# Where the most used form of a run-time switch lies: another order for eight bodies of code

## The chip, the cores and the metric

One core of one Trainium2 chip runs the whole program. TensorE (PE) multiplies matrices; each multiplication stands in the trace as a load of weights (PEld) and a MATMUL. VectorE (DVE), ScalarE (ACT) and GpSimd (POOL) do the elementwise work; SyncE (SP) and POOL start most of the DMA transfers. Each engine has an instruction stream of its own, which is itself fetched from memory by DMA. The metric is the device time of one execution in microseconds (us), lower is better.

## What is computed

Two blocks in a row: an attention in which each position sees the first `n_global` keys and the last `n_local` ones, then a mixture of eight experts in which every token goes to one expert.

```
scores = scale * q @ k.T + bias            # 4 batches, 8 heads, 768 positions, 64 wide
scores = where(is_global | is_local, scores, -1e9)
x = softmax(scores) @ v                    # as 3072 tokens of 512
expert_idx = argmax(x @ w_gate)            # one of 8 experts for each token
for e in range(8):
    xe = x[expert_idx == e]
    out[expert_idx == e] = gate * (relu(xe @ w1[e]) @ w2[e])   # 512 -> 1024 -> 512
```

How many tokens an expert gets is known only at run time, some 384 of the 3072 each.

## The kernel before

The program is straight code with a hand-written order on every engine. The attention and the routing fill the first 170 us or so; rows of tokens are scattered into a buffer in DRAM, sorted by expert. From there on the eight experts follow one another, and this is the part that the change touches.

An expert's tokens are taken in three portions. Experts 0 and 1 have a first tile of 128 rows done early. Each expert then has a main part of 256 rows, which is always computed (`up_a`, `up_b`, `down_a`, `down_b`, in a Strassen-like scheme that needs sums of weights, `c1` and `c2`, made by DVE). What is left over, between 0 and 224 rows in steps of 32, is the *units*: a piece of 128 rows, one of 64 and one of 32, each present or not. So there are eight forms, numbered k = 0 to 7 by the three bits (4: the piece of 128; 2: that of 64; 1: that of 32). k = 5 is the form of 160 rows, k = 4 that of 128, k = 3 that of 96, k = 1 that of 32.

The form is chosen at run time. `table` (the line is quoted below) writes `k ^ ORDER` for every expert; `load_forms` brings the eight numbers into registers of PE and ACT, the only two engines whose code differs by form. `by_form` opens `tc.Switch`: in PE's stream and in ACT's stream there are eight bodies one behind the other, at equal distances, and the body that lies at place p holds the code of form `p ^ ORDER`. A branch at the end of the common code (line 1316 in the profile, the *dispatch*) jumps to the body, and a branch at the body's end (line 1316 too, the *exit*) jumps to the code behind, which is common to all forms again. Between the two branches PE issues the units' matmuls (lines 1107, 791, 801, 1118, 1132), with the main part's `down_a` (line 1025) mixed in; ACT issues the relus and copies that go with them.

```
nc.vector.tensor_scalar(self.form[:], k_i[:], ORDER, None, ALU.bitwise_xor)
```

```
for k in tc.Switch({eng: self.forms[e] for eng in self.ENGINES}, FORMS, hint=f"units{e}"):
    self.units(e, k ^ ORDER, between)
```

`hint(e)` gives PE alone a prefetch hint for the dispatch of expert e. Each body begins with a hint for its own exit, on both engines (line 1148).

Behind the exit of expert e, these follow, and the steps of the prediction name them by line:

- PE: `x_in(e + 1)` (line 943, eight transposes), `down_b(e)` (line 1034), then the next expert's `up_a` and `up_b` (line 963). The first `up_b` adds into the same PSUM bank that `up_a(0)` filled, and waits until DVE's first `up_add` (line 994) has read that bank.
- ACT: `gated` (line 1045, two multiplications of one half of the result by the gate), then the next expert's `up_copy` (line 990).
- DVE: `down_sums` (line 1041), the copies of the next expert's tokens (945), `x_combine` (953 to 956), one `y_out` (1055) that needs `gated`, `c1[3]` (923), three more `y_out` (1055, 1052, 1055), behind expert 1 also the eleven small instructions of `judge` (1268 to 1281), and then the next expert's `up_add` (994).
- POOL: the scatters of finished rows (725) and the gathers of the next ones (717); SP: the next but one expert's weights, 4 MB, into the buffers that expert e has just given up.

Of the kernel before, what the change touches and what calls it, by code (L numbers as in the profile page):

```python
# [23 lines left out]
def kernel(  # L24
# [636 lines left out]
    NS = 2  # L661
    SP1 = 32
    FORMS = 8
    ORDER = 6

    HF = NFC // 2
    HD = NDC // 2
# [3 lines left out]
    class Experts:  # L671
# [177 lines left out]
        def table(self):  # L849
# [29 lines left out]
            nc.vector.tensor_copy(out=k_i[:], in_=k[:])  # L879
            nc.vector.tensor_scalar(self.form[:], k_i[:], ORDER, None, ALU.bitwise_xor)  # L880
            bits_i = T([P, 3, E], I32, name="bits_i")
# [265 lines left out]
        def by_form(self, e, between):  # L1147
            for k in tc.Switch({eng: self.forms[e] for eng in self.ENGINES}, FORMS, hint=f"units{e}"):
                self.units(e, k ^ ORDER, between)
            if e + 1 < E:  # L1150
# [170 lines left out]
```

## Time and profile before

| | us |
|---|---|
| median of 4 runs | 521.41 |
| lowest and highest of them | 520.22 and 523.12 |
| the profiled execution, whole | 522.21 |
| its span in the trace | 520.4 |
| PE busy in the span | 502.0 |
| DVE busy | 327.8 |
| POOL busy | 189.9 |
| ACT busy | 147.4 |

The span is counted from the first to the last recorded instruction, so it is a little shorter than the execution's own time; 1.8 us lie around it. The granted TensorE clock was 0.995 over the span. In the trace the experts can be told by the shapes of the units' matmuls: expert 0 has the form of 96 rows, experts 1 and 7 that of 32, experts 2 and 4 that of 128, and experts 3, 5 and 6 that of 160.

In the timeline a line gives the start, the time from the first instruction's start to the last one's end, the engine, the line of the kernel, the operation with its tiles, a count, and in brackets how long the engine had been idle before and what the profile names as having ended that.

### The profile page before, as it was taken

Reading aid. Unit: us, or ns where it says so; the run is one execution under the profiler, and the core shown is the slowest. Engines: PE = TensorE matmul, PEld = TensorE weight load, DVE = VectorE, ACT = ScalarE, POOL = GpSimd, SP = SyncE. Lnnn points to the kernel's source line nnn. Section 1 sums busy time; section 2 is a strip of 40 time slices with the busy share of each in tenths; the row PEclk is TensorE's granted clock in tenths of the full one; section 3 lists DMA queues with packets and bytes.
Section 4 is the critical chain, followed back from the end, with each engine's and each line's share of the span. In section 5 each row is a group of like instructions: output and inputs, shape, how many; then the busy total and the mean of one; then the engine's idle time right before and its main releaser. Section 6 shows DMA issues by size and latency. Waiting matters only on the chain.

```text
span 520.4 us, 12430 instructions
## 1 busy us (share of the span) xinstructions
PE 502.0 (96%) x5035; PEld 423.7 (81%) x5035; DVE 327.8 (63%) x688; ACT 147.4 (28%) x298; POOL 189.9 (36%) x285
## 2 busy tenths in 40 slices
PE   7999999999996999999999999999999999999994
PEld 4888888888885778679899788969969868996983
DVE  5898998997994647727788168227617705822741
ACT  3554555555542101212212112102202211211120
POOL 5441161161163465315374055024316304502503
PEclk9999999999998999999999999999999999999999
DMA  9977699798941322046093452028164107400101
GB/s 184 210 156 164 163 213 238 162 264 198 360 176 43 122 69 67 9 173 246 21 325 113 162 216 66 2 108 321 40 232 181 26 1 278 160 2 24 42 5 50
DMA packets 96333, 72.77 MB, mean 140 GB/s; under 512 B 79324, under 2 KB 79326, under 8 KB 96228
## 3 DMA queue, kind: packets, MB, share of 16 engines
q1 hardware_dynamic: 87808, 52.44, 36.1%
q0 software_dynamic: 7872, 19.01, 10.7%
q8 instruction: 55, 0.90, 0.8%
q14 instruction: 50, 0.41, 0.3%
q10 hardware_dynamic: 548, 0.02, 0.1%
HBM read 61.46 MB, written 14.73 MB: 146 GB/s over the span
## 4 chain that ended last, share of the span: by engine, by line
PE 78%; DVE 8%; issue 6%; DMA 5%; POOL 1%; POOLq 0%; SPq 0%; ACT 0%; DVEq 0%; ACTq 0%
PE u L963 18%; PE u L791 10%; PE d L1025 9%; PE d L1034 7%; PE u L801 7%; PE po L402 5%; PE sp L360 5%; DMA w<-in_moe_w_dram 3%; DVE p L374 3%; PE d L801 3%; PE u L1132 3%; PE u L1107 2%; PE pt L239 2%; PE pr L412 2%; PE t L943 2%
## 5 line engine op out<-in xcount | busy, mean ns | idle before, releaser
L1041 DVE TENSOR_TENSOR UV<-UV,d 128x512 f32<-128x512 f32 x8 | 5.5, 687 | 110.9 <-ACT yu L1135 81.3
L725 POOL DMA_INDIRECT out_dram<-ys,to_u x8 | 8.3, 1039 | 142.6 <-ACT yu L1135 87.6
L374 DVE TENSOR_TENSOR p<-sp,other 128x1024 f32<-128x1024 f32 x40 | 47.0, 1217 | 12.3 <-PE sp L360 10.8
L791 PEld LDWEIGHTS u<-xsT,w 128*128 128x128 f32 x448 | 50.9, 192 | 1.8 <-DVE c L933 1.2
L791 PE MATMUL u<-xsT,w 128*128 128x128 f32 x448 | 51.7, 276 | 0.0
L402 PE MATMUL po<-p,vt 128*64 128x128 f32 x704 | 47.6, 283 | 2.3 <-DVE kt L244 2.2
L963 PE MATMUL u<-cx,c 128*128 128x128 f32 x384 | 48.1, 275 | 0.0
L402 PEld LDWEIGHTS po<-p,vt 128*64 128x64 f32 x704 | 39.0, 140 | 9.0 <-DVE kt L244 5.0
L381 ACT ACTIVATE p<-p 128x1024 f32<-128x1024 f32 (+1 forms) x48 | 45.0, 978 | 3.9 <-DVE p L374 2.8
L963 PEld LDWEIGHTS u<-cx,c 128*128 128x128 f32 x384 | 45.5, 192 | 0.0
L360 PE MATMUL sp<-qt,kt 64*128 64x128 f32 x448 | 38.1, 276 | 2.3 <-DVE kt L244 1.7
L963 PE MATMUL u<-xT,w 128*128 128x128 f32 x256 | 39.4, 277 | 0.0
L801 PE MATMUL u<-w,huT 128*128 128x512 f32 x80 | 35.1, 592 | 0.0
L963 PEld LDWEIGHTS u<-xT,w 128*128 128x128 f32 x256 | 34.2, 192 | 0.9 <-DVE cx L956 0.2
L360 PEld LDWEIGHTS sp<-qt,kt 64*128 64x128 f32 x448 | 31.1, 188 | 4.1 <-issue 2.3
L296 POOL COPY ka<-kt 128x384 f32<-128x384 f32 x16 | 8.1, 504 | 69.3 <-DVE den_all L436 66.9
L1025 PE MATMUL d<-c,ch 128*128 128x256 f32 x128 | 32.9, 379 | 0.0
L217 POOL DMA_INDIRECT xs_dram<-xr,slot_i x24 | 25.2, 1051 | 16.9 <-DVE cnt L853 11.0
L801 PEld LDWEIGHTS u<-w,huT 128*128 128x128 f32 x80 | 15.2, 190 | 17.0 <-issue 16.7
L242 ACT ACTIVATE qt<-pt 128x512 f32<-128x512 f32 x24 | 14.4, 598 | 51.8 <-PE pt L239 51.8
L390 DVE TENSOR_TENSOR pb<-p 128x512 f32<-128x512 f32 x40 | 28.9, 764 | 0.0
L1025 PEld LDWEIGHTS d<-c,ch 128*128 128x128 f32 x128 | 24.4, 190 | 3.3
(255 smaller groups left out, 1031.2 us busy)
## 6 DMA issues: line engine op xcount, KB each, us to landing
w<-in_moe_w_dram SPq DMA_DIRECT2D x24, 1024.0 KB, 8.5
w<-in_moe_w_dram SPq DMA_DIRECT2D x16, 512.0 KB, 7.3
raw_q<-in_q_dram SPq DMA_DIRECT2D x24, 256.0 KB, 4.4
raw_k<-in_k_dram SPq DMA_DIRECT2D x24, 256.0 KB, 4.9
vt<-in_v_dram SPq DMA_DIRECT2D x24, 256.0 KB, 5.2
xs_dram<-xr,slot_i POOLq DMA_INDIRECT x24, 4.6
xg<-xs_dram,grow POOLq DMA_INDIRECT x16, 6.0
mu<-xs_dram,grow_e POOLq DMA_INDIRECT x16, 2.1
```

The lines of the kernel that those rows point to most:

```text
L217: d = nc.gpsimd.indirect_dma_start(out=xs_dram[:], out_offset=bass.IndirectOffsetOnAxis(ap=slot_i[:, u:u + 1], axis=0), in_=xr[:, u, :].bi ...
L360: nc.tensor.matmul(sp[:, a, j, t, :], lhsT=kt[r, m, :], rhs=qts[n][r, m, :], start=True, stop=True, skip_group_check=True)
L374: nc.vector.tensor_tensor(z, sc, bi, ALU.add)
L381: nc.scalar.activation(z, z, AF.Exp)
L390: nc.vector.tensor_tensor(t[:].rearrange("p a j c -> p (a j) c"), z[:, :, 0, :], z[:, :, 1, :], ALU.add)
L402: nc.tensor.matmul(po[D * a:D * a + D, m % 2, :], lhsT=vt[:, 2 * m + a, :], rhs=ps[n][m // 2][:, a, m % 2, t, :], start=(x == 0), stop=(x ...
L791: nc.tensor.matmul(ph[:, i, :], lhsT=self.w[e % 2][0][:, c, ts(half * HF + i, P)], rhs=xT[:, c, :], start=(c == 0), stop=(c == NDC - 1), s ...
L801: nc.tensor.matmul(py[:].rearrange("p a b -> p (a b)"), lhsT=h[:, f, :], rhs=self.w[e % 2][1][:, f, :], start=(f == 0), stop=(f == NFC - 1 ...
L963: nc.tensor.matmul(bank[:, r, :], lhsT=lhs(k), rhs=rhs(k), start=first, stop=True, skip_group_check=True)
L1025: nc.tensor.matmul(self.half(i, j), lhsT=lhs, rhs=rhs, start=(f == 0 and j == 0), stop=True, skip_group_check=True)
L1034: nc.tensor.matmul(self.half(i, j), lhsT=lhs(f), rhs=rhs(f), start=False, stop=True, skip_group_check=True)
L1132: nc.tensor.matmul(py[n * o:n * o + n, :], lhsT=self.hu[s - 1][:, i, n * g:n * g + n], rhs=w2t[:, m * g + i, ts(o, q)], start=(i == g == 0 ...
```

## The change

One constant, which is used in two places (the two quoted above):

```
     FORMS = 8
-    ORDER = 6
+    ORDER = 2
+
```

The place of form k is `k ^ ORDER`. So the bodies in the order of their places hold:

| place | 0 | 1 | 2 | 3 | 4 | 5 | 6 | 7 |
|---|---|---|---|---|---|---|---|---|
| form before | 6 | 7 | 4 | 5 | 2 | 3 | 0 | 1 |
| form after | 2 | 3 | 0 | 1 | 6 | 7 | 4 | 5 |

Before, the form of 32 rows lies at the end of all, next to the code behind; after, that of 160 rows does. Every body has the same instructions as before, and so has all the code around them; the extra empty line moves the line numbers below it by one.

## The prediction

> **What bounds the kernel now.** I read the page's chain of waits and its DMA queues first, then PE's waits inside the experts (180 to 500 us), then the timeline of ACT, DVE and PE around each exit from the switch.
>
> ```profile
> PE 78%; DVE 8%; issue 6%; DMA 5%; POOL 1%; POOLq 0%; SPq 0%; ACT 0%; DVEq 0%; ACTq 0%
> ...
> q8 instruction: 55, 0.90, 0.8%
> q14 instruction: 50, 0.41, 0.3%
> ```
>
> PE makes the chain. The two instruction queues matter here, since nothing but the place of code changes: q8 moves packets of 16 KB (0.90 MB by 55), at PE's pace; q14 moves packets of 8 KB, for the other engines. In the straight code PE runs 4,594 records over 18 packets, 255 to a packet, so a PE block is 256 instructions and an 8 KB block half of that.
>
> ```profile
> PE t L943 <- issue: 0.9, 4, 0.3
> PE d L801 <- issue: 0.4, 1, 0.4
> ```
>
> These are all of PE's idle gaps between 180 and 500 us: 0.9 us at the code behind the switch, four times, 0.3 at most. PE has nothing to win there. What can be lost is read at the exits on ACT (expert 1, then 3, then 6):
>
> ```profile
> 261.59 0.37 ACT L1135 ACTIVATE yu<-u,gate_u 128x128 f32<-128x128 f32 x1 [2.21 <-PE u L1132]
> 262.77 0.91 ACT L1045 ACTIVATE gu<-UV,gate 128x256 f32<-128x256 f32 x2 [0.81 <-DVE UV L1041]
> ...
> 346.99 0.37 ACT L1135 ACTIVATE yu<-u,gate_u 128x128 f32<-128x128 f32 x1 [1.20 <-PE u L1132]
> 352.24 0.91 ACT L1045 ACTIVATE gu<-UV,gate 128x256 f32<-128x256 f32 x2 [4.88 <-POOL gate L948]
> ...
> 477.23 0.37 ACT L1135 ACTIVATE yu<-u,gate_u 128x128 f32<-128x128 f32 x1 [1.20 <-PE u L1132]
> 479.82 0.91 ACT L1045 ACTIVATE gu<-UV,gate 128x256 f32<-128x256 f32 x2 [2.23 <-DVE xT L945]
> ```
>
> Expert 1's form lies last, and `gated` (L1045) starts 1.12 us after the exit's end, as soon as DVE's sum is there. Expert 3's lies in the middle, and it takes 5.20. The page blames POOL's copy, but in experts 1 and 6 `gated` ran before that copy, so it is not what ACT waits for. An 8 KB packet is: it starts at 350.61 in expert 3 and at 478.14 in expert 6, and `gated` follows 1.2 to 1.3 us behind its end. From exit's end to `gated`, experts 0 to 7: 5.26, 1.12, 4.34, 5.20, 4.06, 5.44, 2.54, 1.12. The two 1.12 are the two experts whose form lies last. The 2.54 is the one far exit without a weight transfer; from 261.9 to 276 us, behind expert 1, the transfer keeps the DMA engines some 90% busy.
>
> ```profile
> 268.34 0.14 DVE L1268 TENSOR_SCALAR okn<-num 128x1 f32<-128x1 f32 x1
> ...
> 270.54 0.41 DVE L994 TENSOR_TENSOR uv<-uv,u 128x256 f32<-128x256 f32 x1
> ...
> 271.31 0.61 PE L963 MATMUL u<-xT,w 128*128 128x128 f32 x4
> ...
> 356.00 0.40 DVE L994 TENSOR_TENSOR uv<-uv,u 128x256 f32<-128x256 f32 x1
> ```
>
> `gated` releases a `y_out` on DVE; behind that in DVE's queue stand c1[3], three more `y_out` and the first `up_add` (L994), for which PE's first `up_b` waits. From L994's end to that matmul there is room, behind experts 0 to 6: 0.06, 0.36, 0.76, 0.41, 0.76, 0.15, 0.76 us. Behind expert 1, DVE also has `judge` in this queue, 2.2 us from 268.34 to 270.54.
>
> **The change part by part.**
>
> *The number in the table, the bodies themselves:* the same instructions, an xor with 2 for 6; 0.
>
> *Dispatch.* PE takes 0.35 to 0.40 us from the branch to the body for places 2, 3, 5 and 7 alike, ACT 2.65 to 3.2 likewise. In expert 7 PE's branch record is 1.84 us long, but its matmuls go 497.61, then 498.56, as they do in expert 1: its queue covered it. 0, for any place.
>
> *PE's exits.* Near (expert 1) 0.30 us, far (2 to 6) 0.30 to 0.32. Experts 1 and 7 become far; the second packet of expert 1's body starts at 254.06 and its exit is at 260.63, in expert 7 502.61 and 507.17, so the code is there. 0. Without that cover it would be an ACT-like 2.5 us.
>
> *ACT's exits in experts 3, 5 and 6* become near: `gated` up to 4.1, 4.3 and 1.4 us earlier. PE was not waiting there (room 0.41, 0.15, 0.76), so 0.
>
> *ACT's exit in expert 7* becomes far: 2.54 for 1.12, no weights moving. `gated` at 510.7 for 509.30, its `y_out` at 511.7 for 510.31, done at 512.2; DVE's next one started at 512.30 anyway, behind PE's `down_b`. 0, with 0.1 us to spare before it shows, and it would have to delay the last `y_out`, at 514.03, to reach the end.
>
> *ACT's exit in expert 1* becomes far, with the weights of expert 3 coming in. Nearest rows: experts 3, 5 and 0, where the transfer starts together with the exit as here: 5.2 to 5.4. `gated` at 261.65 + 5.2 to 5.4 = 266.9 to 267.1. From `gated` to L994's end took 4.19, 4.16, 4.13 us (experts 0, 3, 5); with `judge` 2.2 more: 273.2 to 273.4. PE wants it at 271.31 less 0.06. PE stalls 2.0 to 2.2 us; I take 2.1. Bounds: with 4.06 to 4.34 (experts 4 and 2) 0.7 to 1.1; with 2.54, L994 ends at 270.6, before PE needs it: 0. Above, no far exit took longer than 5.44. What is late next is DVE's own queue: some 0.7 us more behind PE than before, with idle gaps of 0.6 and 0.5 us at 275 to 276 to take it up; c1[3] would be ready at 269.5, needed at 271.75.
>
> *Where the code behind begins.* The change says 152 instructions into a block. If it moved, PE could win no more than the 0.9 us above. I think it does not move. Bodies are 2,246 to 2,250 PE instructions in all for each expert, the code behind 331 to 336: 10 blocks and 17 to 26 more. Were only whole blocks padded in, the place in the block would drift by that for each expert, whatever the order. The trace shows such a drift: behind experts 0 to 5 there are two packets before the next dispatch, behind 6 three, the last at 495.52, 0.7 us before the branch. Extrapolated from the straight code, the code behind begins at 61 to 73 in expert 0, 171 to 183 in expert 5 and 195 to 207 in expert 6, where the second crossing falls 16 to 28 instructions before the branch: that packet. 0.
>
> Sum: 2.1 us on the profiled execution, 522.21 to 524.3. That execution lies 0.8 above the median of the runs, so on the median 521.41 + 2.1 = 523.5.
>
> [...]
>
> **The rivals.**
>
> *Slower: expert 5 asks too late for its next block.* The 160-row body ends 408 instructions on, 152 into its second block; the code behind begins at 171 to 183 of the same block in expert 5. A jump within a block may start no packet: plain jumps of POOL (489.27) and SP (392.62) are followed by none. Then PE asks at the crossing, near 435.1 us. In this profile a packet wanted about then started at 440.41, took 0.97 and would be usable 1.2 later, 442.6; PE's queue runs dry at 438.6 to 439.3. Loss 3.3 to 4.0, and up to 0.9 in expert 6: in all 521.41 + 2.1 + 4.2 = 527.7. It decides if PE's packet behind expert 5 moves from 434.15 to about 440. Against: after ACT's near exit in expert 7 a packet did start (509.16), so a hinted jump seems to start one.
>
> *Nothing reaches PE:* expert 1's packet slips in ahead of the weights, as in expert 6: 521.4. Against: their traffic begins 0.5 us behind that exit.
>
> *The code behind does move, and that helps:* 521.41 - 0.9 = 520.5, or with the stall 522.6. Against: the drift.
>
> **How the numbers follow.** 0.5% is 2.6 us, about what a measurement of this kernel can tell from no change. The forecast, 523.5 and itself 522.4 to 524.3, 0.60; the late block 0.22; nothing reaches PE 0.12; a moved code behind 0.06. The last two and five sixths of the first lie within 0.5%; the late block, a sixth of the first and some of what I have not seen lie above: slower 0.39, same 0.57, faster 0.04. The range goes from 521.0, the case of no effect with some scatter, to 528.0, the late block.
>
> **What would show it.** Behind expert 1, ACT's L1045 near 267 and not 262.77, a gap of about 2 us on PE before the fifth group of L963, and 1.12 us from exit to `gated` in experts 3, 5 and 6. Wrong, if PE's stall stands elsewhere, above all near 439 in expert 5, or if the number of PE's packets behind expert 6 changes.

## The result and the profile after

The changed kernel takes 525.17 us in the median of 45 runs (521.84 to 527.65), the kernel before, on the same chips, 522.74 us in 71 runs (516.72 to 525.94). The ratio is 1.0066, 95% interval 1.0051 to 1.0082: on 522.74 us that is 3.45 us slower (2.7 to 4.3), more than 0.5% and far from 2%. The two medians by themselves lie 2.43 us apart, less than that interval; runs of either kernel scatter by 6 to 9 us.

The two profiled executions hardly differ, 522.50 us and 522.21 us whole, spans 520.7 and 520.4. That misleads: the attention ahead of the experts, which the change doesn't touch, happened to end 4.1 us earlier in the profile after (the first `up_a` of expert 0 starts at 194.46 us, before at 198.60). The profile before has a wait of 2.9 us for rows from DRAM (line 782) and 3.41 us at half of the TensorE clock behind it (granted clock 0.50 from 163.17 to 166.59), and the profile after has neither. Over the profiles of all kernels below this start lies anywhere from 194.46 to 203.00. So I compare the *experts' stretch*, from that first `up_a` to the end of expert 7's up phase (its `up_a` and `up_b`): 298.30 us before, 302.59 after, +4.29.

The page of the changed kernel, its chain of waits and its two instruction queues:

```profile
PE 74%; DVE 14%; issue 9%; POOL 1%; ACT 1%; POOLq 0%; DVEq 0%; ACTq 0%
...
q8 instruction: 55, 0.90, 0.8%
q14 instruction: 49, 0.40, 0.2%
```

q8 has the same 55 packets, q14 one less. I read q8 as the queue of TensorE's code: in the kernel below with 64 more TensorE records (32 LDWEIGHTS and 32 MATMUL) it has 57, and q14 stays at 49. So TensorE's code is fetched in as many packets as before. PE's share of the chain fell; the waits of PE between 180 and 500 us (total, times, longest) say where one entered:

```profile
PE u L964 <- DVE uv L995: 2.2, 2, 1.9
PE t L944 <- issue: 0.9, 4, 0.3
```

The second row is as before. The first is new: the `up_b` that waits for `up_add` (all lines are one higher than before). The timeline of ACT at the exits of experts 1, 3 and 6:

```profile
257.90 0.37 ACT L1136 ACTIVATE yu<-u,gate_u 128x128 f32<-128x128 f32 x1 [2.21 <-PE u L1133]
263.23 0.91 ACT L1046 ACTIVATE gu<-UV,gate 128x256 f32<-128x256 f32 x2 [4.96 <-POOL gate L949]
...
347.14 0.37 ACT L1136 ACTIVATE yu<-u,gate_u 128x128 f32<-128x128 f32 x1 [1.20 <-PE u L1133]
348.32 0.91 ACT L1046 ACTIVATE gu<-UV,gate 128x256 f32<-128x256 f32 x2 [0.81 <-DVE UV L1042]
...
477.32 0.37 ACT L1136 ACTIVATE yu<-u,gate_u 128x128 f32<-128x128 f32 x1 [1.20 <-PE u L1133]
478.50 0.91 ACT L1046 ACTIVATE gu<-UV,gate 128x256 f32<-128x256 f32 x2 [0.81 <-DVE UV L1042]
```

Expert 1's `gated` (263.23) now starts 5.27 us behind its exit instead of 1.12; experts 3 and 6, far before, are near now and start in 1.13. In expert 1 an 8 KB packet of q14 starts at 261.60 and takes 0.31 us, and `gated` follows 1.32 us behind its end. What that does to DVE, first and last instruction of `judge` and then `up_add`:

```profile
264.25 0.48 DVE L1056 SCALAR_TENSOR_TENSOR y<-UV,gate,gu 128x256 f32<-128x256 f32 x1 [2.42 <-ACT gu L1046]
...
266.96 0.14 DVE L1269 TENSOR_SCALAR okn<-num 128x1 f32<-128x1 f32 x1
...
269.19 0.16 DVE L1282 CAST bad_b<-bad 128x1 bf16<-128x1 f32 x1
269.26 0.41 DVE L995 TENSOR_TENSOR uv<-uv,u 128x256 f32<-128x256 f32 x1
```

and to PE in expert 2:

```profile
266.28 1.50 PE L964 MATMUL u<-cx,c 128*128 128x128 f32 x12
269.73 1.14 PE L964 MATMUL u<-xT,w 128*128 128x128 f32 x4 [1.95 <-DVE uv L995]
270.67 1.06 PE L964 MATMUL u<-xT,c 128*128 128x128 f32 x4
271.52 1.06 PE L964 MATMUL u<-cx,w 128*128 128x128 f32 x4
272.37 1.04 PE L964 MATMUL u<-xT,w 128*128 128x128 f32 x4
273.23 1.52 PE L964 MATMUL u<-cx,c 128*128 128x128 f32 x12
274.59 0.61 PE L964 MATMUL u<-xT,w 128*128 128x128 f32 x4
```

PE waits for `up_add` as predicted. What was not predicted stands below the wait: a group of four starts every 0.85 us (270.67 to 271.52) where it was 0.445 before (271.31 to 271.75), up to 273.2. Windows of the same stretch (length, busy time of PE, PEld, DVE, ACT and POOL with counts, then the granted TensorE clock, the DMA share and GB/s):

```profile
264.00:267.50 3.50, 3.50 (x32) 3.47 (x32) 3.18 (x9) 0.51 (x2) 1.57 (x2) 1.00 1.05 384
267.50:269.70 2.20, 0.28 (x3) 0.09 (x1) 2.03 (x10) 0.37 (x1) 1.83 (x4) 1.00 1.03 392
269.70:271.50 1.80, 1.77 (x8) 1.77 (x9) 1.80 (x3) 0.00 (x0) 1.56 (x4) 0.54 1.05 401
271.50:273.30 1.80, 1.80 (x11) 1.80 (x10) 1.73 (x4) 0.42 (x1) 1.22 (x3) 0.51 0.29 108
273.30:277.00 3.70, 3.70 (x35) 3.70 (x35) 1.29 (x4) 0.73 (x2) 0.00 (x0) 1.00 0.01 2
```

The same work in the kernel before ran without idling and at the full clock:

```profile
270.00:274.00 4.00, 4.00 (x39) 4.00 (x38) 3.90 (x10) 0.54 (x3) 3.38 (x4) 1.00 1.04 355
```

TensorE was busy for 0.28 of the 2.20 us from 267.50, and then worked on at half its clock: the granted clock is 0.50 from 269.84 to 273.25. The up phase of experts 0 to 7 was 13.46, 13.57, 13.46, 13.55, 13.46, 13.46, 13.47, 13.46 us before and is 13.46, 14.01, 17.30, 13.55, 13.46, 13.46, 13.46, 13.46 after: +3.84 in expert 2 and +0.44 in expert 1 are the whole 4.29.

In what follows *idling* is the time from where the fifth group would have followed in step (1.79 us behind the start of `up_a(1)`) to its start: in the profile after 269.73 - 265.83 - 1.79 = 2.11 us. It is a little more than the wait that the profile names.

### The profile page after: what moved, and what is told of

The parts are those of the page before. It is cut to its first block, busy times and chain, and to the rows that moved or that the text cites. A ratio compares the mean times of both kernels' runs of the same rounds, so it can differ in the third digit from the quotient of the medians.

```text
span 520.7 us, 12430 instructions
## 1 busy us (share of the span) xinstructions
PE 502.7 (97%) x5035; PEld 424.4 (81%) x5035; DVE 328.6 (63%) x688; ACT 147.4 (28%) x298; POOL 191.5 (37%) x285
## 4 chain that ended last, share of the span: by engine, by line
PE 74%; DVE 14%; issue 9%; POOL 1%; ACT 1%; POOLq 0%; DVEq 0%; ACTq 0%
PE u L964 17%; PE u L792 10%; PE d L1026 9%; PE u L802 7%; PE d L1035 5%; DVE p L374 5%; PE po L402 5%; PE sp L360 4%; PE d L802 3%; PE u L1133 3%; PE u L1108 2%; PE pt L239 2%; DVE pb L390 2%; DVE kt L244 2%; PE pr L412 2%
## 5 line engine op out<-in xcount | busy, mean ns | idle before, releaser
L402 PE MATMUL po<-p,vt 128*64 128x128 f32 x704 | 46.2, 278 | 2.3 <-DVE kt L244 2.2
L402 PEld LDWEIGHTS po<-p,vt 128*64 128x64 f32 x704 | 37.7, 137 | 9.1 <-DVE kt L244 5.0
L991 ACT COPY uv<-u 128x256 f32<-128x256 f32 x32 | 11.9, 372 | 58.1 <-PE u L964 58.0
```

The lines of the kernel that those rows point to most:

```text
L402: nc.tensor.matmul(po[D * a:D * a + D, m % 2, :], lhsT=vt[:, 2 * m + a, :], rhs=ps[n][m // 2][:, a, m % 2, t, :], start=(x == 0), stop=(x ...
```

## The experiments

### Is it expert 1's exit?

First expert 1 alone put back; one more small VectorE instruction writes its column of the table.

```
-    ORDER = 2
+    ORDER, ORDER_1 = 2, 6
...
+            nc.vector.tensor_scalar(self.form[:, 1:2], k_i[:, 1:2], ORDER_1, None, ALU.bitwise_xor)
...
-                self.units(e, k ^ ORDER, between)
+                self.units(e, k ^ (ORDER_1 if e == 1 else ORDER), between)
```

> The changed kernel, with expert 1 alone back in the old order (its 32-row form in the last place), and one more small instruction on VectorE that writes this column of the table. Theory (ScalarE's far exit behind expert 1 makes TensorE wait about 2 us in expert 2, and TensorE then works some 3.5 us at half its clock): the wait and the half-clock stretch are gone, the up phase of expert 2 is 13.46 us again instead of 17.30, and the time against the kernel before is 1.000 to 1.0015 (0.44 us of expert 1 may stay). Rival (another exit, or the place where the code behind begins in a block): the time stays near 1.0066 and the 3.8 us stand elsewhere.

Measured: 526.03 us against 525.58, 1.0009 (0.999 to 1.0027); up phase of expert 2 13.46 us, no wait for `up_add` among PE's waits, experts' stretch 298.35. The loss is gone, though the 160-row form still lies last.

The reverse, `ORDER, ORDER_1 = 6, 2`:

> The kernel before, with expert 1 alone in the new order (its 32-row form in place 3, all other experts as before). Theory: this alone brings the loss: gated 5.2 us behind ScalarE's exit in expert 1, TensorE waiting 2 us ahead of the fifth group in expert 2, up phase of expert 2 near 17.3 us, time 1.005 to 1.008 of the kernel before. Rival (the loss is made by the other experts' exits or by the 160-row form at the end): 1.000, up phase of expert 2 at 13.46.

Measured: 1.0051 (1.0028 to 1.0073); `gated` 5.20 us behind the exit, idling 2.07 us, up phase of expert 2 17.26 us, experts' stretch 302.63. Expert 1's place alone makes the whole loss. Expert 1's own up phase was 13.91 us here with expert 0 in its old place, and 13.61 in the kernel above with expert 0 in its new place, so the 0.44 us of the profile after isn't made by the change.

A third order, `ORDER = 4`, with expert 0's form last and the 160-row form in place 1:

> The kernel before with a third order: each number in the table xored with 4, so that the 96-row form of expert 0 lies last, expert 1's in place 5 (far), the 160-row form in place 1. Theory (expert 1's far exit, judge, and TensorE's idling): the loss is there although the 160-row form isn't last: gated some 5.2 us behind the exit in expert 1, a wait of 1.9 us and half clock in expert 2, its up phase 17.3 us, time 1.005 to 1.008; behind expert 0, whose exit is near now, gated starts 1.1 us behind the exit and expert 1's up phase takes 13.46. Rival (the 160-row form at the end makes the loss): up phase of expert 2 13.46, time 1.000.

Measured: 1.0083 (1.0052 to 1.0114); `gated` 5.25 us behind expert 1's exit and 1.23 behind expert 0's; idling 2.03 us; up phases 13.46 in expert 1 and 17.22 in expert 2; stretch 302.21. The 160-row form at the end isn't needed for the loss.

### Is it judge?

```
-                if e in (1, 2):
-                    judge(e)
+                if e in (3, 4):
+                    judge(e - 2)
```

> The changed kernel, with the two steps of judge behind experts 3 and 4 instead of 1 and 2, the orders as changed. Theory: without judge's 2.2 us in VectorE's queue the first up_add of expert 2 ends at about the time at which TensorE wants it, so that TensorE waits 0 to 0.2 us there and its clock stays full: up phase of expert 2 13.46 to 13.7 us, and 0 behind expert 3, whose exit is near (gated 4 us earlier than before the change); time 1.000 to 1.0015. Rival (ScalarE's late exit alone is enough, whatever stands in VectorE's queue): 1.0066 as the changed kernel.

Measured: 0.9997 (0.998 to 1.0014), stretch 298.24. The timeline of ACT and then of DVE behind expert 1:

```profile
265.28 0.37 ACT L1136 ACTIVATE yu<-u,gate_u 128x128 f32<-128x128 f32 x1 [2.21 <-PE u L1133]
270.80 0.91 ACT L1046 ACTIVATE gu<-UV,gate 128x256 f32<-128x256 f32 x2 [5.15 <-POOL gate L949]
```

```profile
271.81 0.48 DVE L1056 SCALAR_TENSOR_TENSOR y<-UV,gate,gu 128x256 f32<-128x256 f32 x1 [2.60 <-ACT gu L1046]
...
274.14 0.47 DVE L1056 SCALAR_TENSOR_TENSOR y<-d,gate,gu 128x256 f32<-128x256 f32 x1
274.53 0.41 DVE L995 TENSOR_TENSOR uv<-uv,u 128x256 f32<-128x256 f32 x1
```

ACT is as late as in the changed kernel (5.45 us), but `up_add` follows `y_out` at once and ends at 274.94, when PE wants it: up phase 13.56 us. So the far exit alone costs 0.1 us here; it needs `judge` in the same queue. Why a far exit takes ACT over 5 us here and 2.56 behind expert 7 is read from the rows alone (in the changed kernel the DMA share is 0.90 in the 5.27 us behind expert 1's exit, where the weight transfer runs, and 0.04 in the 2.57 us behind expert 7's, where none does); no run took the transfer away.

### Is it idling that halves the clock?

Work in the gap: matmuls into a bank that is overwritten later, 16 of them, then 8 (`range(8)`).

```
                 self.up_sums(1)
+                if e == 2:
+                    for k in range(16):
+                        nc.tensor.matmul(self.u[3][:, k % 4, :], lhsT=self.w[0][0][:, k % HD, 0:P],
+                                         rhs=self.xT[:, k % HD, 0:P], start=(k == 0), stop=True, skip_group_check=True)
                 self.up_b(e, 0)
```

> The changed kernel, with 16 matmuls of 128x128 into a bank that is free then, between the second and the fifth group of expert 2's up phase, whose product is overwritten: 16 x 0.111 = 1.8 us of work where TensorE otherwise idles some 2 us. Theory (the loss is 2.1 us of waiting and 1.7 us of half clock behind it): the wait shrinks to under 0.4 us, the granted clock stays 1.0 behind it, and the up phase of expert 2 with the added matmuls takes 15.4 to 15.8 us instead of 17.30; time 1.002 to 1.005. Rival (the slow matmuls behind the wait come from something else, such as VectorE's or the DMA's traffic at that time): they stay slow, 17.3 us, 1.0066.

Measured: 1.0145 (1.0118 to 1.0172), much worse than expected, from two causes. I had priced a call at 0.111 us, but it makes two records: the 16 took 3.57 us, more than the gap. The up phase was 17.04 us = 13.46 + 3.58, at full clock (1.00 in each window from 270 to 282 us). Further, the added instructions moved all TensorE code behind them by 64, and a new wait opened behind expert 5:

```profile
439.71 0.84 PE L944 MATMUL t<-ident,xg 128*128 128x128 f32 x6 [0.21 <-issue]
443.78 0.58 PE L944 MATMUL t<-ident,xg 128*128 128x128 f32 x2 [3.23 <-issue]
444.16 3.62 PE L1035 MATMUL d<-w,ch 128*128 128x256 f32 x8
447.58 2.62 PE L1035 MATMUL d<-w,h 128*128 128x256 f32 x8
450.03 1.89 PE L1035 MATMUL d<-c,h 128*128 128x256 f32 x8
```

After six transposes TensorE waits 3.23 us for nothing that the profile shows (`issue`), most likely for code (a packet of q8 starts at 441.47 and takes 0.95), and then again runs at half clock (0.50 from 443.70 to 448.00; eight matmuls to the next group's start in 3.42 us, where the last groups take 1.73). From the end of expert 5's up phase to expert 6's first matmul 37.36 us pass, before 31.38. The old order with the same 16 matmuls tells whether the near exit or the code's place in its block is to blame:

> The kernel before with the same 16 added matmuls in expert 2 as the kernel called fill (they made 3.57 us of work, not the 1.8 us expected there, and 64 more TensorE instructions, which move the code behind the switch of the later experts by 64). In fill, TensorE then waited 3.2 us behind expert 5 for code (its packet came at 441.47, 2.8 us behind the exit at 438.68, ACT's and the weight traffic ahead of it) and ran at half clock after. Theory 1 (expert 5's near exit, with the 160-row form last, starts no packet, and the next block lies 9 to 21 instructions on): with the old order expert 5's exit is far, its packet starts with the exit, and the wait behind expert 5 is gone: from expert 5's up phase's end to expert 6's first matmul 31.4 us and not 37.4, time 1.007. Theory 2 (the place of the code in the block alone decides, whatever the order): 37.4 us again, and 1.018.

Measured: 1.0121 (1.0057 to 1.0186, from 3 runs), an interval that holds both theories' times. The trace decides (of the longest of four executions, 534.99 us): 37.91 us again, and TensorE waits behind the same six transposes, 3.5 us for nothing that the profile shows. Theory 1 fell; the order isn't to blame. The packet started 2.78 us behind expert 5's exit in the one and 2.95 in the other, as in the kernels without added work (2.60 after, 2.68 before). What the two have in common is the place: by my estimate, fewer instructions were left in the block to cover the packet. That count is worked out from the 16 KB packets and the 64 added instructions, not seen in the trace.

With 8 matmuls:

> As fill, with 8 added matmuls, 1.78 us by fill's 0.223 us each, and 32 more TensorE instructions. Theory for expert 2: TensorE is busy for most of its wait, so the wait is 0.1 to 0.4 us, the clock stays full, and the up phase takes 13.46 + 1.78 + the wait = 15.3 to 15.7 us, 1.6 to 2.0 less than the changed kernel without added work. Rival (TensorE's idling isn't the cause of half clock): 17.0 or more. Behind expert 5: in fill TensorE ran dry after 6 transposes, 12 instructions; with 32 instructions less it has 44 left to the end of the block, 5.2 us of work from the exit, and code asked for at the exit is usable 4.9 to 5.4 us behind it: wait 0 to 0.3 us, 31.4 to 31.7 us from expert 5's up phase to expert 6's first matmul. Behind expert 6, 23 instructions are left: wait 0.2 to 0.6 us. Time 1.002 to 1.005.

Measured in expert 2, as expected:

```profile
273.81 1.06 PE L1166 MATMUL u<-xT,w 128*128 128x128 f32 x8
275.02 0.71 PE L964 MATMUL u<-xT,w 128*128 128x128 f32 x4 [0.15 <-DVE uv L995]
275.57 0.61 PE L964 MATMUL u<-xT,c 128*128 128x128 f32 x4
```

A wait of 0.15 us, full clock, up phase 15.67 us. That is 1.63 us less than the changed kernel takes with less work. The time, 1.0087 (1.0063 to 1.0111), missed: the 32 instructions lost it elsewhere. Behind expert 5's exit there was no 3 us wait, as worked out, but expert 5's dispatch branch took 3.36 us, and PE waited behind it and behind expert 6 for nothing that the profile shows (`issue`, 1.2 us at line 1108 and 1.6 in two waits at line 1035), so most likely for code: from the end of the up phase to the next expert's first matmul 33.47 us for expert 5 and 32.83 for expert 6, against 31.38 and 31.39.

Then idling with nothing else changed: in the kernel before, n VectorE operations of 128x256 f32 behind `judge` in expert 1.

```
                 if e in (1, 2):
                     judge(e)
+                if e == 1:
+                    for _ in range(4):
+                        nc.vector.tensor_tensor(junk[:], junk[:], junk[:], MAX)
...
+        junk = const.tile([P, 256], F32, name="junk")
+        nc.vector.memset(junk[:], 0.0)
```

> The kernel before, with three added VectorE operations of 128x256 f32 (some 0.42 us each, by the like rows of the kernel before) behind judge in expert 1, so that the first up_add of expert 2 ends 1.26 us later: less the room of 0.36 us TensorE idles 0.9 us. Theory (idling itself halves TensorE's clock): what follows shows from which length on; with 1.9 us it did. If 0.9 us is enough, the up phase of expert 2 takes 13.46 + 0.9 + 1.7 = 16.1 us, if not 14.4 us (1.0017). Rival (the half clock belongs to the far exit or to the weight transfer, not to idling): 14.4 us here and just the added wait in all the delays.

> As the kernel with three, with four added operations: TensorE idles 1.3 us. Theory: up phase of expert 2 14.8 us if 1.3 us of idling leaves the clock alone, 16.5 us if it halves it. Rival: 14.8 us.

> As the kernel with three, with eight added operations: TensorE idles 3.0 us, with no exit of the switch changed. Theory: the granted clock falls to half behind it for some 3.5 us, and the up phase of expert 2 takes 13.46 + 3.0 + 1.7 = 18.2 us, time 1.008 to 1.010 of the kernel before. Rival (half clock not made by idling): 16.5 us, 1.006.

> As the kernel with four added VectorE operations (1.41 us of idling, clock full), with five: TensorE idles 1.8 us, against the 1.9 us of the changed kernel at which the clock fell. Theory: up phase of expert 2 15.4 us if the clock holds, 17.1 us if it falls; either narrows the bound between 1.41 and 1.90 us. Rival (idling isn't what counts): 15.4.

Measured, with the three kernels in which the exit makes the wait among them:

| kernel | idling, us | up phase of expert 2 | less 13.46 and the idling | time, ratio |
|---|---|---|---|---|
| 3 operations | 0.95 | 14.52 | 0.11 | 1.0041 (1.0002 to 1.0079) |
| 4 | 1.41 | 14.98 | 0.11 | 1.003 (0.9994 to 1.0066) |
| 5 | 1.92 | 15.49 | 0.11 | 1.0029 (1.0011 to 1.0046) |
| order with 4 | 2.03 | 17.22 | 1.73 | 1.0083 (1.0052 to 1.0114) |
| expert 1 alone far | 2.07 | 17.26 | 1.73 | 1.0051 (1.0028 to 1.0073) |
| the changed kernel | 2.11 | 17.30 | 1.73 | 1.0066 (1.0051 to 1.0082) |
| 8 | 3.31 | 18.50 | 1.73 | 1.0106 (1.0066 to 1.0147) |

Windows of the kernel with 5 operations, then with 8:

```profile
271.56:273.48 1.92, 0.16 (x2) 0.00 (x0) 1.82 (x6) 0.37 (x1) 1.62 (x4) 1.00 1.03 325
273.48:277.00 3.52, 3.52 (x31) 3.52 (x32) 3.41 (x6) 0.51 (x2) 2.85 (x5) 1.00 0.75 298
```

```profile
268.30:271.60 3.30, 0.16 (x2) 0.00 (x0) 3.09 (x9) 0.37 (x1) 2.82 (x6) 1.00 1.06 403
271.60:275.10 3.50, 3.49 (x16) 3.49 (x17) 3.42 (x6) 0.42 (x1) 1.23 (x2) 0.51 0.37 143
275.10:279.00 3.90, 3.90 (x37) 3.90 (x36) 1.49 (x6) 0.79 (x2) 0.00 (x0) 1.00 0.00 0
```

With 5 the clock column stays 1.00, with 8 it is 0.51 for 3.5 us and then 1.00, without any change at an exit. So idling was enough: behind 3.31 us of it the clock was halved. In the table the clock holds up to 1.92 us of idling and falls from 2.03 on, in one execution of each kernel; the times form the same two groups, but their intervals overlap.

The length alone does not decide, and the other stretches of these traces show it. In each of the 13 profiles the instants at which the granted clock changes lie whole multiples of 3.413 us apart: in the kernel before 157.01 us = 46 x 3.413 and 351.57 us = 103 x 3.413, in the changed kernel 262.83 us = 77 x 3.413 and 245.76 us = 72 x 3.413, with 8 operations 256.00 us = 75 x 3.413 and 245.76 us. I count on from them through each trace in steps of 3.413 us, call an instant so counted an edge and the stretch between two a window. Where the windows begin differs between the traces: in the first two below an edge lies at 155.49 and at 155.99. One wait in the attention, of 2.6 us ahead of line 402, shows what goes with that. It ends so in the kernel with 16 added matmuls, in the one with `judge` moved and in the one with expert 1 put back:

```profile
156.62 1.09 PE L402 MATMUL po<-p,vt 128*64 128x128 f32 x16 [2.61 <-ACT qt L242]
...
156.55 3.34 PE L402 MATMUL po<-p,vt 128*64 128x128 f32 x32 [2.62 <-issue]
...
156.19 1.09 PE L402 MATMUL po<-p,vt 128*64 128x128 f32 x16 [2.62 <-issue]
```

The windows of the first, then of the second:

```profile
152.08:155.49 3.41, 1.93 (x16) 1.56 (x15) 1.64 (x2) 0.21 (x1) 2.63 (x5) 1.00 0.42 161
155.49:158.91 3.42, 1.90 (x30) 1.69 (x32) 2.26 (x7) 2.75 (x4) 0.95 (x1) 1.00 0.40 155
158.91:162.32 3.41, 3.41 (x65) 2.92 (x62) 3.31 (x13) 0.64 (x2) 0.88 (x2) 1.00 0.02 7
```

```profile
152.58:155.99 3.41, 1.35 (x12) 1.07 (x10) 2.20 (x2) 0.18 (x1) 2.64 (x4) 1.00 0.52 199
155.99:159.41 3.42, 2.86 (x28) 2.89 (x30) 2.28 (x8) 2.67 (x4) 0.39 (x1) 0.50 0.31 120
```

In the first the edge at 155.49 cuts the wait: PE is idle for 1.48 us of one window and 1.52 of the next, and the clock holds at 1.00. In the second it is idle for 2.06 us of one window, and the whole next window runs at half clock (0.50). So it does in the third, where an edge leaves 1.92 us of idling in one window:

```profile
154.63:158.04 3.41, 1.49 (x24) 1.28 (x26) 2.30 (x5) 2.60 (x4) 1.10 (x2) 1.00 0.43 162
158.04:161.46 3.42, 3.42 (x46) 2.64 (x44) 3.32 (x12) 0.79 (x3) 0.78 (x1) 0.50 0.01 2
```

It is alike in expert 2. Counted in the window with the most of it, the idle time was 1.87 us (order with 4), 1.91 (expert 1 alone far), 1.95 (the changed kernel) and 3.16 (8 operations) where the clock fell to 0.50, and 0.79, 1.18 and 1.49 (3, 4 and 5 operations) where it held. With 5 operations the edge at 273.21 cuts the wait, so whether its 1.92 us would have halved the clock inside one window isn't shown. Nor is an exact limit: in the first 14 us of these profiles the clock fell behind windows with 1.51 to 1.66 us of idle time and held behind 1.61 (in the changed kernel behind 1.50, from 10.43 to 13.84), and near the end of an execution it held once behind 1.99. Some 1.5 to 2 us in one window is an estimate from these. And since the windows lie differently in the profiled executions, the profiles don't tell in how many of the 45 runs of the changed kernel the clock fell behind the stall.

No version beat the kernel before. With nothing waiting for `up_add` there (stretch 298.30 us, at best 298.24) none of the three orders tried had more to give.

## Why the prediction was right, and where it was short

The chain of causes held in each link from ACT's exit to PE's stall, and 525.17 us lies in the range on record (521.0 to 528.0). That says little by itself: the range is 7 us wide and holds the 522.74 us of the kernel before too. The size was short: I forecast 523.5 on 521.41, a ratio of 1.0040, which lies below the interval, and the forecast's own range (522.4 to 524.3) does not hold the time. Most of the chance stood on a change within 0.5%, and it is slower than that.

- *Expert 1's exit:* predicted 5.2 to 5.4 us, measured 5.27. From `gated` to the end of `up_add`, predicted 4.13 to 4.19 and 2.2 for `judge`, measured 269.68 - 263.23 = 6.45. PE's stall, predicted 2.0 to 2.2, measured 2.11 (1.95 by the row).
- *The term that was mis-sized:* "What is late next is DVE's own queue", with "Sum: 2.1 us". I took TensorE's rate behind the stall as given. Late next was TensorE itself: it ran 3.4 us at half clock, and the term of 2.1 measured 3.84 in the profiled execution. On 522.74 us that is a ratio of 1.0073, inside the interval. That 521.41 + 3.84 = 525.25 comes so near to 525.17 is chance: the kernel before took 1.33 us more in the later runs than in the four shown then.
- *Experts 3, 5, 6 near, 0:* `gated` 1.13 us behind the exit in all three, the up phases behind them 13.46 before and after or within 0.01. Held.
- *Expert 7, 0:* `gated` 2.56 us behind the exit. The experts' stretch ends ahead of this exit and can't tell, but the last `y_out` ends 17.61 us behind the end of expert 7's up phase both before and after. Held.
- *Dispatch and PE's exits, 0:* far exits took 0.29 to 0.32 us; expert 0's took 1.09, but 0.63 to 1.31 over all kernels, with its old place and its new one alike. Held.
- *The code behind does not move, 0:* the same 55 packets, behind expert 6 at 477.46, 481.10 and 495.46 (before 477.42, 481.13, 495.52). Held; that rival is out.
- *The late block behind expert 5:* the packet started at 434.18, before at 434.15, so it did not happen. Its condition was wrong: with either order the first packet starts 2.6 to 3.0 us behind that exit. A wait at that place was seen in another kernel: with sixteen added matmuls it was 3.23 us long, 3.5 with the old order, and it cost 6.0 and 6.5 us rather than the predicted 3.3 to 4.0, since the half clock came on top there too.
- *Nothing reaches PE:* out; the packet started at 261.60, 3.6 us behind the exit's end, and didn't slip in ahead.

How long the half clock lasted is read off the windows: (1 - granted clock) x 2 x length gives 1.66 + 1.76 = 3.4 us in the changed kernel and 3.4 with 8 operations. With 16 added matmuls it was 6.83 us behind expert 5, where the first of two windows at half clock was idle for 1.57 us. At the rate I took as given, the stall would have cost its 2.1 us alone; by the rows it cost 3.84.

## What to carry to other kernels

Price a stall of TensorE by its length and by the clock behind it: here 1.92 us cost 2.03, and 2.03 us cost 3.76. In expert 2 the clock behind it went with how much of the stall fell into one window of 3.41 us (it held up to 1.49 us and fell from 1.87 on), and the same wait of 2.6 us in the attention left the clock at 1.00 in one execution and halved it in two others. Here a late exit on an engine off the critical path was paid for by what else stood in the queue behind it: 0.1 us without `judge` there, 3.84 with it; the repair that worked here was to move work that nothing waits for soon (`judge`) to where the queue has room. And where attention or anything ahead scatters by 8 us between executions, compare the stretch that the change can reach, not two spans.

## What was not expected of the hardware

- The step of the clock: 0.11 us of extra loss up to 1.92 us of idling, 1.73 from 2.03 us to 3.31, the same in all four cases; by the granted clock in their windows the half clock lasted 3.4 us in each. The same wait of 2.6 us in the attention left the clock alone where a window's edge cut it into 1.48 us and the rest, and halved it in two executions that had 1.92 and 2.06 us of idling in one window.
- What added TensorE instructions cost elsewhere: 64 of them 6.0 us behind expert 5, 32 of them 2.1 there and 1.4 behind expert 6, with the same work at the places where it was lost. That the place of the code in memory did it is my reading of the `issue` waits there. A test that adds instructions measured this too, so it is read by its place in the trace and not by its time.
